# Pair scores from 32 sums and differences and a constant matrix, on two row groups of the array

## The chip, the core and the metric

The kernel runs on one core of one Trainium2 chip. The metric is the device time of one execution in microseconds (us); less is better. The program names the engines as the profile does: PE is TensorE's matmuls, PEld its weight loads, ACT is ScalarE, DVE is VectorE, POOL is GpSimd, SP is SyncE.

## The reference

The input is x (4 batches of 12416 tokens of 128 channels), 32 inducing vectors and three weights. Attention goes twice through a small set of 32 vectors, and a gated block follows:

```python
h = mab(I, x)                      # 32 inducing rows attend to all tokens of a batch
return mab(x, h)                   # each token attends to the 32 rows of h
...
gate = np.maximum(x @ w_gate, 0.0)
val = x @ w_val
return gate * val @ w_out          # d_ff is 1536
```

Here `mab(q, kv)` is `softmax(q @ kv.T / sqrt(128)) @ kv`.

## The kernel before

**The algebra.** A token's attention weights p over the 32 rows of h are positive and sum to 1. Where the sign of each of the 1536 gates is the same for all tokens, the output is a quadratic form in p: a sum over pairs (k, m) of p_k p_m times a vector of 128 outputs. The product of two exponentials is the exponential of the sum of two scores. So the kernel takes 16 x 32 = 512 sums of two rows of h (`hs`), computes 512 pair scores for each token by a matmul of x with `hs`, exponentiates them (F), and multiplies F by a table T of 512 rows. A further set of 16 sums and 16 differences of rows (`h2`, made by `halves`, L125) gives 32 more exponentials per token (`p2`), which meet rows 512 and up of T: the fifth product. A column of T adds up the softmax's denominator. A guard, `general_kernel`, does the plain computation where the signs are not certain; it isn't run on these inputs.

**Tiles.** A batch has 97 token tiles of 128, which form 24 blocks of four tiles (512 tokens) and one tile more. Four blocks make a chunk: six chunks and the last tile.

**Stages.** `first_batch` (L153) loads x of batch 0, transposes it on PE, and computes h. Then comes a hand-written order of gates, products and tables of batch 0 (L940 to L969). After it one loop over all 4 x 97 tiles (L1004) emits everything else. For each block: two score units (`scores`, L555), each two matmuls of 128x512 into the two halves of an `e_ps` tile (L581) and one exponential of 128x1024 on ACT (L588). For each token tile: four products of F with T and the fifth product, all into one third of an `o_ps` bank (`outputs`, L592: L602, L606). After three tiles, DVE takes the reciprocal of the denominators (L621) and scales the rows into `osb` (L622), and POOL stores six tiles by one DMA (L632). [...] two `e_ps` tiles of two banks, two `o_ps`, and two of tag "m" for all else.

For each chunk `mix_p` (L641) computes the 32 scores for four blocks by four matmuls on four column groups (`s2_pe`, L366), exponentiates them on ACT into `p2`, and lets DVE find their largest value (L646). `bound1` to `certain` use it for the guard.

**The next batch.** Between these, the loop does the first attention of the next batch: loads of x (POOL's queue), transposes by DMA (SP's queue) or, for three chunks of batch 1, by PE with a DVE copy (`turn_pe`, L722), scores and sums (L731, L740), h, the gates (`gates_pe`, L340; `gates_out`, L353), products U on DVE (L465), and five tables (L514, L533).

**What sets the order.** There is no scheduler at run time: each engine executes its instructions as they were emitted. The loop at L1003 keeps an estimated clock of each engine and emits next what it thinks can start first: a score unit (`emit_scores`), a side step (`emit_side`) from one of the lanes "phase", "units" and "scores", each with a place measured in half blocks and estimated costs, or the next output tile (`emit_tile`). Loads, transposes and stores are tied to the start of a block (`dmas`). Score units may run up to eight blocks ahead of the outputs (eight F buffers of 4x512).

Of the kernel before, what the change touches and what calls it, by code (L numbers as in the profile page):

```python
# [26 lines left out]
def quadratic_body(ctx, tc, x, inducing, moe_w_gate, moe_w_val, moe_w_out, out):  # L27
# [4 lines left out]
    P = 128  # L32
# [41 lines left out]

    T = [constp.tile([P, 8, P + 2], FP16, name=f"T{i}") for i in range(2)]
# [45 lines left out]
    def new_range(b):  # L121
        state[b]["rng"] = mt([P, 7], FP32, "rng", 2)
        nc.gpsimd.memset(state[b]["rng"], 0.0)

    def halves(b, h_ps, z_ps):  # L125
# [6 lines left out]
        h = s["h"] = st([P, M + NS], FP32, "h", 2)  # L132
# [20 lines left out]
    def first_batch(sp, psum):  # L153
# [30 lines left out]
        warm = mt([P, BLK], FP16, "p2", 14)  # L184
# [42 lines left out]
        new_range(0)  # L227
# [20 lines left out]
        def score(j):  # L248
            t0, t1 = parts[j]
            n = t1 - t0  # L250
            ps = bank("g", "s1_ps", [P, 8, M])
            tile = mt([P, BLK], FP16, "p2", 14)
            if j == 0:
                nc.vector.memset(tile[:, n * M : 8 * M], 0.0)
            for t in range(n):
                nc.tensor.matmul(ps[:, t, :], xTs(xT, t0 + t, 1), indT, start=True, stop=True)  # L256
            p1s[j] = tile[:, 0 : 8 * M].rearrange("p (t m) -> p t m", m=M)
            nc.scalar.activation(  # L258
                out=p1s[j][:, 0:n, :], in_=ps[:, 0:n, :], func=AF.Exp, scale=sm_scale
            )  # L260
# [65 lines left out]
    def h_sums(b):  # L326
        s = state[b]
        s["hs"] = st([P, NS, M], FP16, "hs", 2)
        h = s["h"]
        dve.tensor_copy(out=h[:, M : M + NS], in_=h[:, 0:NS])  # L330
        a = h[:, 0:M]
        wins = bass.AP(a.tensor, a.offset, [a.ap[0], (1, NS), (1, M)])
        dve.tensor_tensor(
            out=s["hs"],
            in0=h[:, 0:M].unsqueeze(1).broadcast_to([P, NS, M]),
            in1=wins,
            op=ALU.add,
        )

    def gates_pe(b, w):  # L340
        ps = bank("e", "hw_ps", [P, 2, BLK])
        for t in range(NFF):
            k, i = divmod(t, NFF // 2)
            nc.tensor.matmul(
                ps[:, k, i * (M + NS) : (i + 1) * (M + NS)],
                w[:, t * P : (t + 1) * P],
                state[b]["hT"],
                start=True,
                stop=True,
            )  # L350
        return ps

    def gates_out(eng, ps, dst, k):  # L353
# [4 lines left out]
        to = dst.rearrange("p (k i) m -> p k i m", k=2)[:, :, :, 0:n]  # L358
# [20 lines left out]
    def bound1(b):  # L379
# [3 lines left out]
        dve.tensor_reduce(out=v, in_=s["rng"], axis=AX.X, op=ALU.max)  # L383
# [130 lines left out]
    def table(b, j):  # L514
# [5 lines left out]
        dve.tensor_copy(out=T[b % 2][:, j, 0:P], in_=ps)  # L520
# [31 lines left out]
    F, p2s, osbs = {}, {}, {}  # L552
    dmas = defaultdict(list)

    def scores(g, half):  # L555
        b, n = divmod(g, NSLOT)
        s = state[b]
        hs = s["hs"].rearrange("p k m -> p (k m)")
        ps = bank("e", "e_ps", [P, 2, BLK])
        if n == NBLK:  # L560
            F[g] = mt([P, 4, BLK], FP16, "F", 8)
            for j in range(4):
                nc.tensor.matmul(
                    ps[:, 0, j * P : (j + 1) * P],
                    hs[:, j * P : (j + 1) * P],
                    xTs(s["xT"], NT - 1, 1),
                    start=True,
                    stop=True,
                )
            act.activation(  # L570
                out=F[g][:, :, 0:P],
                in_=ps[:, 0, :].rearrange("p (j c) -> p j c", j=4),
                func=AF.Exp,
                scale=sm_scale2,
            )
            return
        if half == 0:
            F[g] = mt([P, 4, BLK], FP16, "F", 8)
        for d in range(2):
            j = 2 * half + d  # L580
            nc.tensor.matmul(  # L581
                ps[:, d, :],
                hs[:, j * P : (j + 1) * P],
                xTs(s["xT"], n * TPB, TPB),
                start=True,
                stop=True,
            )
        act.activation(  # L588
            out=F[g][:, 2 * half : 2 * half + 2, :], in_=ps, func=AF.Exp, scale=sm_scale2
        )  # L590

    def outputs(b, t):  # L592
        i = t % 3
        n, tt = divmod(t, TPB)
        g = b * NSLOT + n
        if i == 0:
            outputs.ps = bank("o", "o_ps", [P, 3, P + 1])
        ps = outputs.ps[:, i, :]
        r = n % 4
        tok = slice(tt * P, (tt + 1) * P)  # L600
        for j in range(4):
            nc.tensor.matmul(  # L602
                ps, F[g][:, j, tok], T[b % 2][:, j, 0 : P + 1], start=j == 0, stop=False
            )
        rows = slice(0, P if n < NBLK else M)
        nc.tensor.matmul(  # L606
            ps,
            p2s[b, n // 4][rows, tok],
            T[b % 2][rows, 4 + r, 0 : P + 1],
            start=False,  # L610
            stop=True,
        )
        done = i == 2 or t == NT - 1
        if done:
            k = i + 1
            a = t - i
            if a % 6 == 0:
                osbs[0] = mt([P, 6, P], FP32, "osb", 4)
            osb, a6 = osbs[0], a % 6
            rz = mt([P, 3, 1], FP32, "rzo", 4)  # L620
            dve.reciprocal(out=rz[:, 0:k, :], in_=outputs.ps[:, 0:k, P : P + 1])  # L621
            dve.tensor_tensor(  # L622
                out=osb[:, a6 : a6 + k, :],
                in0=outputs.ps[:, 0:k, 0:P],
                in1=rz[:, 0:k, :].broadcast_to([P, k, P]),
                op=ALU.mult,
            )
            if a6 == 3 or t == NT - 1:
                t0 = a - a6
                last = b == B - 1 and t >= NT - 8  # L630
                queue = pool if not last else act if t == NT - 1 else nc.sync
                store = lambda: queue.dma_start(  # L632
                    out=ov[b][:, t0 : t + 1, :], in_=osb[:, 0 : t + 1 - t0, :]
                )
                if last:
                    store()
                else:
                    dmas[g + 1].append(store)
        return done

    def mix_p(b, q, later=False):  # L641
        ps = bank("m", "s2_ps", [P, BLK])
        k, w = s2_pe(b, q, ps)
        p2 = p2s[b, q] = mt([P, BLK], FP16, "p2", 14)
        act.activation(out=p2[0:k, 0:w], in_=ps[0:k, 0:w], func=AF.Exp, scale=sm_scale2)  # L645
        reach = lambda: dve.tensor_reduce(  # L646
            out=state[b]["rng"][0:k, q : q + 1],
            in_=ps[0:k, 0:w],
# [4 lines left out]
        if later:  # L653
            return reach
        reach()


# [7 lines left out]
    def charge(steps, tag=None, after=0.0):  # L665
        t = after
        if tag:
            i = taken[tag] % 2
# [10 lines left out]
    lanes = {"phase": [], "units": [], "scores": []}  # L679
# [7 lines left out]
    def plan_scores(b):  # L687
        h0 = 2 * NSLOT * b
        for q in range(0 if b else 1, NCH):
# [3 lines left out]
                h0 - 3 + 2.5 * q,  # L693
                lambda q=q: mix_p(b, q),
                [("PE", 0.32 * w), ("ACT", 0.5 * w), ("DVE", 0.64 * w)],
                "m",
                ("p2", b, q),
                [("h", b)],
            )
        later("scores", h0 + 15, lambda: bound1(b), D(0.6), None, ("b1", b))  # L700
        later(
            "scores",
            h0 + 16,
# [6 lines left out]
        later("scores", h0 + 17, lambda: certain(b), D(0.5), None, ("certain", b), [("A", b)])  # L710

    def plan_phase1(b):
# [9 lines left out]
        def turn_pe(q, k):  # L722
# [6 lines left out]
            dve.tensor_copy(out=s["xT"][q][:, 8 * k : 8 * k + 8, :], in_=ps)  # L729
# [54 lines left out]
        def h_end2():  # L784
            halves(b, s["h_ps"][:, 0, :], s["h_ps"][:, 1, :])
            new_range(b)
# [14 lines left out]
        if b == 1:  # L801
            moved["in"], moved["turn"] = 4.0, 0.0
            dmas[0] += [lambda q=q: turn(q) for q in turns[0:4]]
            for h in range(6):
# [4 lines left out]
                    [("PE", 0.47), ("DVE", 0.7)],  # L809
# [34 lines left out]
        def gates(w, a, odd, eng, eng2):  # L844
            ps = gates_pe(b, w)
            gates_out(eng, ps, a, 0)
            gates_out(eng2, ps, odd, 1)

        later(
            "phase",  # L850
            c + 2,
            lambda: gates(wg, ga, gb, act, act),
            [("PE", 0.35), ("ACT", 0.65), ("ACT", 0.65)],
            "e",
            ("g", b),
            [("h", b), ("T", b - 1)],
        )
        later("phase", c + 2.5, f(h_sums), D(0.86), None, ("hs", b), [("h", b)])
        later(
            "phase",  # L860
            c + 3.5,
            lambda: gates(wv, va, vb, dve, act),
            [("PE", 0.35), ("DVE", 0.7), ("ACT", 0.65)],
            "e",
            ("v", b),
        )
# [21 lines left out]
        for j, k in enumerate(ends):  # L888
            todo.append(
                (place(k) + 1.5, f(table, j), [("PE", 0.7), ("DVE", 0.3)], "m", ("T", b, j), [("U", b, k)])  # L890
# [27 lines left out]
    done.update({("h", 0): 0.0, ("hs", 0): 0.0, ("T", 0): 0.0, ("p2", 0, 0): 0.0})  # L918
# [3 lines left out]
    for b in range(B):  # L922
# [4 lines left out]
        2 * (n_all - NSLOT) + 20,  # L927
# [8 lines left out]
    def all_k(t0):  # L936
        for i, odd in ((0, 0), (1, 0), (1, 1), (0, 1)):
            products(i, t0, 3, 0, NS, odd)

    ps = gates_pe(0, wg)  # L940
    gates_out(act, ps, ga, 0)
    ps2 = gates_pe(0, wv)
    gates_out(act, ps2, va, 0)
    gates_out(act, ps, gb, 1)
    gates_out(act, ps2, vb, 1)
    h_sums(0)
    gate_sum(0, 0)
    signs(0)
    reach = mix_p(0, 0, True)
    all_k(0)  # L950
    masked_act(0, 0, 3)
    scores(0, 0)
    masked_act(0, 3, 3)
    scores(0, 1)
    table_all(0, 0, 3)
    masked_act(0, 6, 6)
    scores(1, 0)
    all_k(3)
    table_all(0, 3, 3)
    scores(1, 1)  # L960
# [5 lines left out]
    table5(0)  # L966
    table_all(0, 9, 3)
    scores(2, 0)
    reach()  # L969


    NF = 8
# [289 lines left out]
```

## Time and profile before

| what | value |
|---|---|
| median of 6 runs | 303.12 us (299.46 to 306.18) |
| the profiled execution's own time | 299.69 us |
| its span, first to last instruction | 297.6 us |
| mean granted TensorE clock | 0.996 |
| first score exponential starts, last one starts | 27.9 us, 280.7 us |
| last fifth product starts | 290.7 us |
| moved by DMA | 48.37 MB |

In a row of a group, the numbers behind the bar are the time in which the engine was busy with the group and the mean length of one instruction in ns, then the idle time ahead of the group and what ended most of it. A row of the timeline has the start, the length from the first start to the last end, and the number of instructions merged into it. Matmuls overlap, so the length of one is not the time between two.

The span in 40 slices of 7.4 us:

```
PE   4997999999897999998999999989999999999991
DVE  3659865547886776778967763669988655664571
ACT  3337899997984778997877889799777889979800
DMA  7999969697979984997999521212423232222253
```

### The profile page before, as it was taken

The page shows a single profiled execution, that of the slowest core. Times are in us where ns is not written, and L with a number is a line of the kernel's source. Part 1 is how long each engine was busy: PE and PEld are TensorE (multiplying, and loading weights), DVE is VectorE, ACT ScalarE, POOL GpSimd, SP SyncE. Part 2 cuts the span into 40 slices and gives each one's busy share as a digit, 9 for nine tenths or more (in the row PEclk, how much of TensorE's full clock was granted, in tenths as well). Part 3 has the DMA queues.
Part 4 walks back from the last instruction along what each step waited for, and adds up shares of the span by engine and source line. Part 5 has one row for each costly group of instructions (what it writes and reads, how often), then busy time and mean ns, then how long its engine had stood idle before and what let it go on. Part 6 is the DMA issues. An engine that isn't in the chain of part 4 may idle for free.

```text
span 297.6 us, 9408 instructions
## 1 busy us (share of the span) xinstructions
PE 275.9 (93%) x4029; PEld 206.5 (69%) x4029; DVE 202.6 (68%) x561; ACT 228.1 (77%) x290; POOL 61.9 (21%) x134
## 2 busy tenths in 40 slices
PE   4997999999897999998999999989999999999991
PEld 2884877677666787765777787666778776667790
DVE  3659865547886776778967763669988655664571
ACT  3337899997984778997877889799777889979800
POOL 7461000223211013311302012011211121121220
PEclk9999999999999999999999999999999999999998
DMA  7999969697979984997999521212423232222253
GB/s 181 202 208 207 215 90 245 126 226 142 260 212 233 179 186 122 208 265 222 220 173 285 177 108 64 106 57 107 161 86 129 107 118 109 103 111 108 106 214 126
DMA packets 44433, 48.37 MB, mean 163 GB/s; under 512 B 35472, under 2 KB 36272, under 8 KB 44384
## 3 DMA queue, kind: packets, MB, share of 16 engines
q0 software_dynamic: 11936, 38.08, 47.1%
q1 hardware_dynamic: 32160, 9.16, 18.0%
q8 instruction: 33, 0.54, 0.8%
q10 hardware_dynamic: 288, 0.46, 0.5%
q14 instruction: 16, 0.13, 0.1%
HBM read 27.80 MB, written 25.43 MB: 179 GB/s over the span
## 4 chain that ended last, share of the span: by engine, by line
PE 61%; ACT 17%; DMA 10%; DVE 7%; issue 2%; SPq 0%; POOL 0%; ACTq 0%; DVEq 0%; POOLq 0%
PE o_ps L602 23%; PE e_ps L581 19%; ACT F L588 15%; PE o_ps L606 5%; DMA x<-in_x_dram 5%; DMA x16r<-in_x_dram 3%; PE T_ps L517 3%; DVE U L471 2%; PE s_ps L736 2%; DMA xT<-x 2%; PE hz_ps L757 2%; PE s_ps L370 2%; DVE osb L622 1%; ACT p L645 1%; PE T_ps L537 1%
## 5 line engine op out<-in xcount | busy, mean ns | idle before, releaser
L588 ACT ACTIVATE F<-e_ps 128x1024 f16<-128x1024 f32 x192 | 187.3, 1031 | 29.7 <-PE e_ps L581 27.7
L602 PE MATMUL o_ps<-T,F 128*128 128x129 f16 x1552 | 132.0, 221 | 1.9 <-DVE osb L622 1.6
L602 PEld LDWEIGHTS <-F 128*128 128x128 f16 x1552 | 106.1, 98 | 31.4 <-issue 4.8
L581 PE MATMUL e_ps<-xT,hs 128*128 128x512 f16 x384 | 106.2, 378 | 2.8 <-ACT gb L360 1.7
L606 PE MATMUL o_ps<-T,p 128*128 128x129 f16 x388 | 84.6, 218 | 0.0
L632 POOL DMA_DIRECT2D out_dram<-osb x65 | 35.5, 546 | 205.7 <-DVE osb L622 148.6
L622 DVE TENSOR_TENSOR osb<-o_ps,rzo 128x384 f32<-128x384 f32 x132 | 72.5, 549 | 4.5
L581 PEld LDWEIGHTS <-hs 128*128 128x128 f16 x384 | 32.1, 97 | 22.5 <-issue 8.2
L621 DVE RECIPROCAL rzo<-o_ps 128x3 f32<-128x3 f32 x132 | 23.1, 175 | 27.2 <-PE o_ps L606 25.7
L606 PEld LDWEIGHTS <-p 128*128 128x128 f16 x388 | 37.9, 98 | 0.4
L646 DVE TENSOR_REDUCE rng<-s_ps 128x1 f32<-128x512 f32 (+1 forms) x28 | 17.7, 631 | 20.2 <-ACT p L645 20.2
L645 ACT ACTIVATE p<-s_ps 128x512 f16<-128x512 f32 (+1 forms) x28 | 15.9, 569 | 1.7 <-PE s_ps L370 1.6
L738 ACT ACTIVATE p<-s_ps 128x512 f16<-128x512 f32 (+1 forms) x21 | 11.8, 577 | 3.9 <-PE s_ps L736 3.8
L258 ACT ACTIVATE p<-s_ps 128x256 f16<-128x256 f32 (+3 forms) x16 | 5.3, 332 | 10.5 <-PE s_ps L256 10.5
L736 PE MATMUL s_ps<-indT,xT 128*128 128x32 f16 x288 | 10.0, 177 | 2.5 <-DMA xT<-x 2.3
L246 DVE COPY xT<-xT_ps 128x1024 f16<-128x1024 f16 (+2 forms) x15 | 8.8, 584 | 5.2 <-PE xT_ps L245 3.8
L736 PEld LDWEIGHTS <-xT 128*128 128x128 f16 x288 | 9.0, 96 | 3.0 <-DMA xT<-x 2.5
L480 DVE TENSOR_TENSOR U<-U,U 128x1536 f16<-128x1536 f16 (+1 forms) x12 | 10.8, 903 | 0.2
L85 POOL DMA_DIRECT2D x<-in_x_dram x18 | 9.8, 551 | 2.1 <-PE s_ps L256 1.3
L768 DVE TENSOR_TENSOR hz<-hz,hz_ps 128x129 f32<-128x129 f32 (+1 forms) x18 | 5.2, 288 | 7.2 <-PE hz_ps L757 6.8
L517 PE MATMUL T_ps<-wo,U 128*128 128x128 f16 x144 | 10.0, 219 | 0.0
L370 PE MATMUL s_ps<-xT,h 128*32 128x512 f16 x96 | 9.6, 389 | 0.0
(153 smaller groups left out, 241.5 us busy)
## 6 DMA issues: line engine op xcount, KB each, us to landing
out_dram<-osb POOLq DMA_DIRECT2D x62, 384.0 KB, 3.3
x<-in_x_dram POOLq DMA_DIRECT2D x18, 512.0 KB, 9.9
x<-in_x_dram POOLq DMA_DIRECT2D x8, 256.0 KB, 7.6
out_dram<-osb SPq DMA_DIRECT2D x2, 384.0 KB, 2.9
x<-in_x_dram POOLq DMA_DIRECT2D x5, 128.0 KB, 8.4
osb<-in_x_dram ACTq DMA_DIRECT2D x1, 384.0 KB, 4.5
osb<-in_x_dram SPq DMA_DIRECT2D x1, 384.0 KB, 4.3
wg<-in_moe_w_gate_dram POOLq DMA_DIRECT2D x1, 384.0 KB, 8.3
```

What stands on the lines that cost most here:

```text
L370: nc.tensor.matmul(ps[32 * r : 32 * r + 32, 0:w], state[b]["h2"], xTs(state[b]["xT"], (4 * q + r) * TPB, w // P), start=True, stop=True,)
L517: nc.tensor.matmul(ps, u_cols(0, t, j), wo[:, t, :], start=t == 0, stop=t == NFF - 1)
L581: nc.tensor.matmul(ps[:, d, :], hs[:, j * P : (j + 1) * P], xTs(s["xT"], n * TPB, TPB), start=True, stop=True,)
L588: act.activation(out=F[g][:, 2 * half : 2 * half + 2, :], in_=ps, func=AF.Exp, scale=sm_scale2)
L602: nc.tensor.matmul(ps, F[g][:, j, tok], T[b % 2][:, j, 0 : P + 1], start=j == 0, stop=False)
L606: nc.tensor.matmul(ps, p2s[b, n // 4][rows, tok], T[b % 2][rows, 4 + r, 0 : P + 1], start=False, stop=True,)
L621: dve.reciprocal(out=rz[:, 0:k, :], in_=outputs.ps[:, 0:k, P : P + 1])
L622: dve.tensor_tensor(out=osb[:, a6 : a6 + k, :], in0=outputs.ps[:, 0:k, 0:P], in1=rz[:, 0:k, :].broadcast_to([P, k, P]), op=ALU.mult,)
L632: store = lambda: queue.dma_start(out=ov[b][:, t0 : t + 1, :], in_=osb[:, 0 : t + 1 - t0, :])
L645: act.activation(out=p2[0:k, 0:w], in_=ps[0:k, 0:w], func=AF.Exp, scale=sm_scale2)
L646: reach = lambda: dve.tensor_reduce(out=state[b]["rng"][0:k, q : q + 1], in_=ps[0:k, 0:w], axis=AX.X, op=ALU.max, apply_absolute_value=True,)
L736: nc.tensor.matmul(ps[:, t, :], s["xT"][q][:, t, :], indT, start=True, stop=True)
```

## The change

The pair scores come no longer from x. With a and b the sums and differences of rows (the 32 scores that `s2_pe` computes), the sum of two row scores is a fixed combination of them. So:

- a constant matrix `sel` (128 x 16 x 32, fp16; the same 32 rows four times) is built once, ahead of the warming matmuls, and takes the place of `hs`;
- `mix_p` falls into `pair_scores` (the four column matmuls), `pair_out` (DVE clamps the scores to +-64 and copies them to SBUF as fp16, `sc`, then finds the largest of that copy) and `pair_exp` (ACT, which now reads `sc`);
- a score unit is now a quarter j of the pairs for two blocks: two matmuls with 32 rows each, on row groups 2d and 2d+1, into the two halves of `e_ps`. F is kept in 16 buffers of 2x512;
- the fifth products of three tiles are emitted together after their twelve others, and, where a score unit is ready then, narrow (32 rows, on the row group of their block) between its two matmuls and its exponential. Otherwise they come as before, on all 128 rows;
- the gates go through "m" banks in halves, even columns copied by ACT and odd ones by DVE; the copies of PE transposes and of table parts move from DVE to ACT; the planner has a lane "exps" and other places and costs.

```diff
+        half = mt([P, M + NS], FP32, "half", 1)
+        for k, op in ((0, ALU.add), (1, ALU.subtract)):
+            nc.vector.tensor_tensor(
+                out=half[:, k * H : (k + 1) * H], in0=stackI[:, 0:H], in1=stackI[:, H:M], op=op
+            )
+        nc.vector.tensor_scalar(
+            out=half[:, 0:M], in0=half[:, 0:M], scalar1=0.5, scalar2=1.0, op0=ALU.mult, op1=ALU.mult
+        )
+        nc.vector.tensor_copy(out=half[:, M : M + NS], in_=half[:, 0:H])
+        windows(sel, half)
-        warm = mt([P, BLK], FP16, "p2", 14)
+        warm = mt([P, BLK], FP16, "p2", 6)
...
-        dve.tensor_copy(out=T[b % 2][:, j, 0:P], in_=ps)
+        act.copy(out=T[b % 2][:, j, 0:P], in_=ps)
...
-    def scores(g, half):
...
-        for d in range(2):
-            j = 2 * half + d
-            nc.tensor.matmul(
-                ps[:, d, :],
-                hs[:, j * P : (j + 1) * P],
-                xTs(s["xT"], n * TPB, TPB),
...
+    def scores(b, q, d, j, within=None):
         ps = bank("e", "e_ps", [P, 2, BLK])
+        sc = scs[b, q]
...
+        for r in range(0 if q == NQ else 2):
+            rows = slice(32 * (2 * d + r), 32 * (2 * d + r) + 32)
+            nc.tensor.matmul(ps[:, r, :], sel4[rows, j, :], sc[rows, :], start=True, stop=True)
+        if within:
+            within()
...
+        F[b, q, d, j] = mt([P, 2, BLK], FP16, "F", NF)
+        act.activation(out=F[b, q, d, j], in_=ps, func=AF.Exp, scale=sm_scale2)
...
+    def fifth_one(b, u, narrow, stop):
+        n, q, r, tok = place_of(u)
+        rows = slice(32 * r, 32 * r + 32) if narrow else slice(0, P if n < NBLK else M)
+        nc.tensor.matmul(
+            outputs.ps[:, u % 3, :],
+            p2s[b, q][rows, tok],
+            T[b % 2][rows, 4 + r, 0 : P + 1],
+            start=False,
+            stop=stop,
+        )
...
+    def fifths(b, t):
+        us = range(t - t % 3, t + 1)
+        blocks = [u // TPB for u in us]
+        main = max(set(blocks), key=blocks.count)
+        wide = [u for u in us if u // TPB != main]
+        for u in wide:
+            fifth_one(b, u, False, False)
+        rest = [u for u in us if u // TPB == main]
+        return rest, lambda narrow: [fifth_one(b, u, narrow, u == rest[-1]) for u in rest]
...
+    def pair_out(b, q, kw, ps):
+        (k, w), s = kw, state[b]
+        sc = scs[b, q] = mt([P, BLK], FP16, "sc", 3)
+        dve.tensor_scalar(
+            out=sc[0:k, 0:w], in0=ps[0:k, 0:w], scalar1=64.0, scalar2=-64.0, op0=ALU.min, op1=ALU.max
+        )
+        if q == 0:
+            s["reach"] = mt([P, NCH], FP32, "reach", 2)
+            pool.memset(s["reach"], 0.0)
+        dve.tensor_reduce(
+            out=s["reach"][0:k, q : q + 1],
+            in_=sc[0:k, 0:w],
...
+    def pair_exp(b, q):
+        k, w = (P, BLK) if q < NQ else (M, P)
+        p2s[b, q] = mt([P, BLK], FP16, "p2", 6)
+        act.activation(
+            out=p2s[b, q][0:k, 0:w], in_=scs[b, q][0:k, 0:w], func=AF.Exp, scale=sm_scale2
+        )
...
-            dve.tensor_copy(out=s["xT"][q][:, 8 * k : 8 * k + 8, :], in_=ps)
+            act.copy(out=s["xT"][q][:, 8 * k : 8 * k + 8, :], in_=ps)
...
+        def gates(w, a, odd, k):
+            ps = bank("m", "hw_ps", [P, BLK])
+            gates_pe(b, w, k, ps)
+            units = slice(k * (NFF // 2), (k + 1) * (NFF // 2))
+            gates_out(act, ps.unsqueeze(1), a[:, units, :], 0)
+            gates_out(dve, ps.unsqueeze(1), odd[:, units, :], 1)
...
+        t_e = unit_ready(begun)
+        rest, issue = fifths(b, t)
+        clock["PE"] += 0.06 * (i + 1 - len(rest))
+        if t_e > clock["PE"] + WAIT or units[e_at][1] == NQ:
+            issue(False)
+            clock["PE"] += 0.06 * len(rest)
+        else:
+            emit_scores(lambda: issue(True))
+            e_at += 1
+        outputs_end(b, t)
```

## The prediction

> **What bounds the kernel now.** I read the shares of busy time first, then the chain that ended last, the costliest groups, the table of waits, and last the timeline of TensorE alone.
>
> ```profile
> PE 275.9 (93%) x4029; PEld 206.5 (69%) x4029; DVE 202.6 (68%) x561; ACT 228.1 (77%) x290; POOL 61.9 (21%) x134
> ...
> PE 61%; ACT 17%; DMA 10%; DVE 7%; issue 2%; SPq 0%; POOL 0%; ACTq 0%; DVEq 0%; POOLq 0%
> ...
> L588 ACT ACTIVATE F<-e_ps 128x1024 f16<-128x1024 f32 x192 | 187.3, 1031 | 29.7 <-PE e_ps L581 27.7
> L602 PE MATMUL o_ps<-T,F 128*128 128x129 f16 x1552 | 132.0, 221 | 1.9 <-DVE osb L622 1.6
> L581 PE MATMUL e_ps<-xT,hs 128*128 128x512 f16 x384 | 106.2, 378 | 2.8 <-ACT gb L360 1.7
> L606 PE MATMUL o_ps<-T,p 128*128 128x129 f16 x388 | 84.6, 218 | 0.0
> ```
>
> TensorE carries 61% of the chain, and ScalarE's exponentials wait for it (27.7 us), hardly ever the reverse. Busy PE is not its price, because matmuls overlap. The price is the step from one start to the next, which the merged rows of the timeline give (row length less the mean of one, by the count less one):
>
> ```profile
> 43.52 0.59 PE L581 MATMUL e_ps<-xT,hs 128*128 128x512 f16 x2
> 44.05 0.40 PE L370 MATMUL s_ps<-xT,h 128*32 128x512 f16 x4
> 44.38 0.41 PE L602 MATMUL o_ps<-T,F 128*128 128x129 f16 x4
> 44.63 0.22 PE L606 MATMUL o_ps<-T,p 128*128 128x129 f16 x1
> ...
> 290.41 0.40 PE L602 MATMUL o_ps<-T,F 128*128 128x129 f16 x4
> 290.74 0.23 PE L606 MATMUL o_ps<-T,p 32*128 32x129 f16 x1
> ```
>
> A 512-column step is 0.59 - 0.378 = 0.215 us; an output product is (0.40 - 0.221)/3 = 0.059, a fifth product 0.056. Four 128*32 matmuls on four column groups take 0.40 together, so they run beside each other. The change of array shape has a price of its own: the second L581 starts at 43.735 and is streamed at 43.95, but L370 starts at 44.05; the last L370 starts near 44.06 and is streamed at 44.28, but L602 starts at 44.38. Each change costs about 0.10. The last row is the same for rows: the fourth L602 starts at 290.59, is through at 290.64, and the 32-row product starts at 290.74: 0.10 again.
>
> With these steps over the program's order TensorE needs 263 us of the 297.6 us span: 91.6 output products (1552 x 0.059), 82.6 scores (384 x 0.215), 21.9 fifths (388 x 0.0565), 10.4 for 104 changes of shape, and 56 for the rest. ScalarE, back to back, needs 220 (an exponential 0.93: ten of them stand in one row of 9.35 us). These two sums are close already.
>
> [...] No run here shows two row groups at once[...]
>
> **The change part by part.** Counts are from the built program's order.
>
> TensorE:
> - Scores: 384 full matmuls become 192 pairs on two row groups: 192 x (0.430 - 0.217) = -40.9. [...] I take 0.217.
> - Fifths: 257 of 388 come narrow inside a unit (105 units), 131 stay full. "A third row group beside them" holds only for 155 of the 257: the score unit runs ahead by a varying number of half chunks, and for 102 the fifth's own row group is one of the pair's, so it queues behind it. 155 x 0.0565 = -8.8. The 102 save nothing; if their weights also load exposed (0.098, the LDWEIGHTS row of L606), 43 units x 0.1 = +4.3; were they hidden too, -5.8. I take 0.
> - Changes of shape: 104 become 416, as nearly each unit goes in and out of row shape: 312 x 0.10 = +31.2. This eats most of the gain.
> - Sum -18.5 by these terms; the whole order costs 243.9 against 263.0, -19.1.
>
> ScalarE: six xT copies (128x1024, as an exponential, 0.93) +5.6; twelve table copies (128x128; L258's row of that shape has 0.277, of which 0.09 overlaps) +2.3; 28 pair exponentials now read SBUF[...]; nine gate copies of 0.65 become twelve halves of 0.42: -0.9. Sum +8: 220 becomes 228.
>
> VectorE: 28 clamped copies from PSUM (va's 576 elements take 0.753, so 512 take 0.69) +17.7; the reductions stay (0.69, from SBUF now); odd gate copies 12 x 0.45 = +5.4; setting up the matrix +1.3. Away: hs -3.5, xT copies -4.1, T casts -3.5, va -2.3. Sum +11: 214 of some 283 us, 76%, so it hides, except where it is the last link: a score unit now waits for PE s2, then DVE's copy. With three sc buffers the copy is placed about 7 blocks ahead, and output rows queue behind it for 1.4 us, while two o_ps banks cover 1.4 us (twice 12 products of 0.059). POOL's memset of reach now sits right ahead of the reduction, behind POOL's stores and loads; four times, 0 to 1 us each; I take 0.
>
> The start: the matrix is built ahead of the warming memset (3.64 us), so warm matmuls begin 1.3 later; the matmul queue is free again at about 7.1, not 5.8, where x's first cast ends at 5.9. Later the start waits for DMA (9.27 us in the chain from 8.1). Bounds 0 and 1.3; I take 0.7. The store, load and transpose DMAs keep their block and their order on POOL and SP; new is only that xT is no longer read by scores, so buffers free earlier.
>
> What the gain is worth: I added both engines over stretches of 12 score units, in both orders. From the 12th unit on, the larger of the two summed to 225.3 before, plus 8.5 of TensorE after the last unit; after the change it is 215.5 plus 3.0. So 19.1 shrinks to 15.3, since ScalarE is now the longer one in 8 of these 16 stretches (3 before). Before, the trace has 247.7 us for that part (43.3 to 291.0), that is 13.9 of waits over 233.8. With as many waits left the span is 297.6 - 15.3 + 0.7 = 283.0. Waits may grow, because in 12 of 16 stretches the two engines lie within 1 us of each other (8 of 16 before), each pair of e_ps banks is a hand-over, and three engines are near full: +0 to +18. They may shrink by up to 12: the 27.7 us that ScalarE waits would be fed by a faster PE. I take 0. The profiled run stood 2.1 us above its span: 285.1. The median of the runs shown is 1.1% above the profiled run's 299.69: 288.
>
> **Rivals.**
> 1. *ScalarE packs densely* (about 275). TensorE's spare time lets scores run just ahead, and ScalarE's 228 us bind: its gate copies start at 24.4, about 222 of its 228 follow, plus half of the old waits (14) and some 9 us of last products and stores: span near 270. For it: ten exponentials back to back at 35.87. Against: the same chain has whole batches of PE, tables and gates.
> 2. *The coupling takes it* (about 302). TensorE waits for a free e_ps bank in unit order, VectorE's copies delay the o_ps banks, and 15 us of new waits stand where TensorE's work was. For it: three sums of 244, 228 and 214. Against: the waits now are small, 0.5 for e_ps on ScalarE and 1.6 for o_ps on VectorE.
> 3. *Row groups don't run beside each other* (about 326; slower). A pair then costs 0.430: 192 x 0.213 = +40.9, the changes of shape stay, and TensorE's sum is 285 against 263: span near 320. It decides from a pair of 0.297 us on, where 192 x 0.08 uses up the 15.3. Against: four column groups share 0.40 us.
> 4. *The transfers bind*: the chain has 15.6 us of x loads and transposes from 75.28 to 91. Up to the 48th unit the stretch sums hardly change (73.4 before, 75.7 after), so batch 0 doesn't reach that wait earlier, and its extra 2.3 us may hide there. Within the range of the first case.
>
> **How the numbers follow.** My forecast (with 4 in it) has 0.65, with an own range of 280 to 297; rival 1 has 0.14, rival 2 0.13, rival 3 0.08. The range, 274 to 303, cuts most of rival 3 and the ends of 1 and 2. What this kernel can tell from no change is about 1% (300.1 to 306.2 here). Faster by over 1%: 0.65, 0.14 and a third of rival 2, 0.83 in all; within 1%: 0.08; slower: 0.09.
>
> **What would show it.** Two rows of L568 starting within 0.01 us, and the pair's step near 0.22: the pairing; 0.43 would be rival 3. The start of each unit 0.10 after the last product is through, likewise its end: changes of shape. Fifths within the pair's 0.38 us where the group is free, after it where not. ScalarE's share up from 77% to over 82%, and its wait for e_ps below 27.7 us. If that wait grows or o_ps waits on VectorE come to several us, rival 2. I am wrong in size if the changes of shape cost much less at row shape in a stream, or if waits move by over 10 us.

## The result, and the profile after

| | before | after |
|---|---|---|
| median of all executions | 302.51 us (71, 298.17 to 307.8) | 302.68 us (34, 296.28 to 310.63) |
| ratio after/before | | 0.9937, interval 0.9907 to 0.9967 |
| profiled execution, its span | 299.69, 297.6 us | 306.29, 304.3 us |
| mean granted TensorE clock of it | 0.996 | 0.922 |
| first reciprocal of batch 0 (end of the start) | 22.74 us | 23.74 us |

The ratio leaves out the slower executions of each kernel (27 of 39 after), so it isn't the quotient of the medians. The forecast of 288 us missed: the change gains 0.6% by this ratio and nothing by the medians, where 5% was forecast.

The clock row of the 40 slices before:

```profile
PEclk9999999999999999999999999999999999999998
```

The page of the kernel after, in the order of the page before: shares of busy time, the clock row, the chain, the groups.

```profile
PE 273.7 (90%) x4029; PEld 192.1 (63%) x4029; DVE 212.4 (70%) x577; ACT 234.5 (77%) x311; POOL 61.3 (20%) x134
...
PEclk9998799955599996579999999999999999999997
...
PE 63%; DVE 16%; ACT 13%; issue 5%; POOL 1%; POOLq 0%; ACTq 0%; DVEq 0%
...
L577 ACT ACTIVATE F<-e_ps 128x1024 f16<-128x1024 f32 x192 | 187.5, 1033 | 30.4 <-PE e_ps L568 29.0
L591 PE MATMUL o_ps<-T,F 128*128 128x129 f16 x1536 | 128.8, 228 | 5.0 <-DVE osb L628 3.7
...
L568 PE MATMUL e_ps<-sc,sel 32*128 32x512 f16 x384 | 76.5, 410 | 4.8 <-ACT won L457 2.4
...
L598 PE MATMUL o_ps<-T,p 32*128 32x129 f16 (+1 forms) x388 | 52.2, 224 | 0.0
```

The score matmuls (L568) take 76.5 us in place of 106.2, and the fifths 52.2 in place of 84.6; yet TensorE's busy time, in which overlapping groups count once, is only 2.2 us less. The chain has more PE than before, no DMA, and VectorE with 16%. ScalarE's wait for scores is 29.0 us, no shorter than the 27.7 before. And the row PEclk, which was 9 in all slices but the last before, has 5s, a 6 and some 7s: the granted clock fell to half for three stretches, 27.9 to 34.8, 62.1 to 82.6 and 116.7 to 133.8 us.

The timeline of TensorE at the place that the prediction used for its steps:

```profile
42.09 0.40 PE L591 MATMUL o_ps<-T,F 128*128 128x129 f16 x4
42.41 0.39 PE L568 MATMUL e_ps<-sc,sel 32*128 32x512 f16 x2
42.42 0.34 PE L598 MATMUL o_ps<-T,p 32*128 32x129 f16 x3
42.74 0.41 PE L591 MATMUL o_ps<-T,F 128*128 128x129 f16 x4
...
43.88 0.22 PE L598 MATMUL o_ps<-T,p 128*128 128x129 f16 x1
44.03 0.39 PE L568 MATMUL e_ps<-sc,sel 32*128 32x512 f16 x2
44.26 0.27 PE L598 MATMUL o_ps<-T,p 32*128 32x129 f16 x2
44.47 0.70 PE L591 MATMUL o_ps<-T,F 128*128 128x129 f16 x9
```

Everything that the prediction said of the array is there. At 42.41 two L568 start within 0.01 us and both are through in one length; three fifths start beside them at 42.42; the next full product starts 0.33 after the pair, which is 0.215 and a change of shape of 0.10. At 44.03 the fifths' row group is one of the pair's, and they start only when it is through, at 44.26.

So I split the time from each start on TensorE to the next into three: what the step costs at full clock by the prediction's prices, what half clock adds to it, and the rest, which is waiting. The split is an estimate: with slightly other prices its differences move by about 1 us.

| profiled run, us | own steps | half clock | waits | before the first and after the last matmul | span |
|---|---|---|---|---|---|
| before | 264.0 | 2.0 | 20.8 | 10.9 | 297.6 |
| after | 245.1 | 17.5 | 29.6 | 12.0 | 304.3 |
| difference (rounded) | -18.9 | +15.5 | +8.8 | +1.1 | +6.7 |
| forecast | -19.1 | 0 | +3.8 | +0.7 | -14.6 |

TensorE's own work shrank as forecast. It was given back by the clock, and by waits. The profiled run had a low clock; over the 39 executions of the kernel after whose clock is on record, the mean clock ran from 0.914 to 0.973 (mean 0.942), and a line through their times is 292.4 us + 181 x (1 - clock), with a correlation of -0.90. At 0.988, the mean of 44 executions of the kernel before, that gives 294.6; since no execution of the kernel after had a clock over 0.973, this is an extrapolation. By it, the clock took about 8.3 us of the median, and another 6 or so of the 14.7 us miss was there at any clock.

### The profile page after: what moved, and what is told of

Same layout as the page of the kernel before. It is cut to its first block, busy times and chain, and to the rows that moved or that the text cites. A ratio compares the mean times of both kernels' runs of the same rounds, so it can differ in the third digit from the quotient of the medians.

```text
span 304.3 us, 9528 instructions
## 1 busy us (share of the span) xinstructions
PE 273.7 (90%) x4029; PEld 192.1 (63%) x4029; DVE 212.4 (70%) x577; ACT 234.5 (77%) x311; POOL 61.3 (20%) x134
## 4 chain that ended last, share of the span: by engine, by line
PE 63%; DVE 16%; ACT 13%; issue 5%; POOL 1%; POOLq 0%; ACTq 0%; DVEq 0%
PE o_ps L591 25%; PE e_ps L568 14%; ACT F L577 10%; DVE osb L628 4%; PE o_ps L598 4%; DVE U L470 3%; PE T_ps L516 3%; PE s_ps L763 2%; PE hz_ps L784 2%; PE s_ps L369 2%; PE T_ps L502 2%; PE xT_ps L259 2%; DVE rzo L627 1%; ACT xT L756 1%; DVE sc L655 1%
## 5 line engine op out<-in xcount | busy, mean ns | idle before, releaser
L591 PE MATMUL o_ps<-T,F 128*128 128x129 f16 x1536 | 128.8, 228 | 5.0 <-DVE osb L628 3.7
L591 PEld LDWEIGHTS <-F 128*128 128x128 f16 x1536 | 94.8, 100 | 36.8 <-issue 19.4
L568 PE MATMUL e_ps<-sc,sel 32*128 32x512 f16 x384 | 76.5, 410 | 4.8 <-ACT won L457 2.4
L598 PE MATMUL o_ps<-T,p 32*128 32x129 f16 (+1 forms) x388 | 52.2, 224 | 0.0
L568 PEld LDWEIGHTS <-sel 32*128 32x128 f16 x384 | 18.5, 92 | 26.5 <-issue 8.7
L598 PEld LDWEIGHTS <-p 32*128 32x128 f16 (+1 forms) x388 | 28.9, 96 | 5.8 <-issue 1.4
L655 DVE TENSOR_SCALAR sc<-s_ps 128x512 f16<-128x512 f32 (+1 forms) x28 | 17.5, 626 | 3.9 <-PE s_ps L369 3.8
L765 ACT ACTIVATE p<-s_ps 128x512 f16<-128x512 f32 (+1 forms) x21 | 11.4, 548 | 10.4 <-PE s_ps L763 10.3
L661 DVE TENSOR_REDUCE reach<-sc 128x1 f32<-128x512 f16 (+1 forms) x28 | 17.6, 627 | 1.4 <-POOL reach L660 0.2
L672 ACT ACTIVATE p<-sc 128x512 f16<-128x512 f16 (+1 forms) x28 | 16.5, 589 | 0.0
```

Of the source, the lines that this page charges most:

```text
L568: nc.tensor.matmul(ps[:, r, :], sel4[rows, j, :], sc[rows, :], start=True, stop=True)
L591: nc.tensor.matmul(outputs.ps[:, i, :], f, T[b % 2][:, j, 0 : P + 1], start=i + j == 0, stop=False)
L598: nc.tensor.matmul(outputs.ps[:, u % 3, :], p2s[b, q][rows, tok], T[b % 2][rows, 4 + r, 0 : P + 1], start=False, stop=stop,)
L655: dve.tensor_scalar(out=sc[0:k, 0:w], in0=ps[0:k, 0:w], scalar1=64.0, scalar2=-64.0, op0=ALU.min, op1=ALU.max)
L661: dve.tensor_reduce(out=s["reach"][0:k, q : q + 1], in_=sc[0:k, 0:w], axis=AX.X, op=ALU.max, apply_absolute_value=True,)
L672: act.activation(out=p2s[b, q][0:k, 0:w], in_=scs[b, q][0:k, 0:w], func=AF.Exp, scale=sm_scale2)
```

## The experiments

Three readings of the clock were on trial. A: it follows how much of the array is streaming, so that a product on 32 rows counts for less than a full one. B: it follows gaps alone, in which TensorE streams nothing. C: it follows the number of waits and hand-overs, which the change raised.

**1. Streams of one shape.** TensorE alone; all of the reference's work is left out. Each stretch below follows one of 110 full products.

```
rows(110, (0,))                     # one row group, no gap
rows(110, (0, 1))                   # pairs on two row groups
strip(110)                          # 128x32, one column group
6 x (full(2), rows(16, (0,)))       # mixed
6 x (full(5), rows(13, (0,)))
```

> Only TensorE streams of 512 columns, one after the other, none of the reference's work: full array, one row group (32 rows), full, two row groups in pairs, full, one column strip (32 columns), full, six times 2 full and 16 of one row group, full, six times 5 full and 13 of one row group, full. Theory A (the granted clock follows the share of the array's cells that stream in windows of 3.41 us, and halves below about a third: in the profile of after the windows with 0.20, 0.30 and 0.31 were followed by half the clock, those with 0.36 and 0.37 were not): one row group (0.25 of the cells, without any gap) falls to 0.5, so does the strip (0.25); pairs (0.5) keep 1.0; 2 of 18 full (0.32 with the changes of shape) falls, 5 of 18 full (0.44) does not. Theory B (the clock falls where TensorE has too many gaps): 1.0 in all streams, since none has a gap.

The answer by stretches (from and to, the length, busy time of PE, PEld, VectorE and POOL with counts, then the granted clock):

```profile
7.00:31.00 24.00, 24.00 (x108) 10.59 (x106) 0.00 (x0) 0.00 (x0) 1.00 0.00 1
37.00:73.00 36.00, 36.00 (x86) 12.20 (x83) 0.00 (x0) 0.00 (x0) 0.50 0.00 0
99.00:123.00 24.00, 24.00 (x222) 10.66 (x222) 0.00 (x0) 0.00 (x0) 1.00 0.01 1
147.00:170.00 23.00, 23.00 (x108) 10.38 (x107) 0.00 (x0) 0.00 (x0) 1.00 0.00 1
...
205.00:241.00 36.00, 36.00 (x83) 10.70 (x82) 0.00 (x0) 0.00 (x0) 0.50 0.00 0
276.00:302.00 26.00, 26.00 (x61) 7.84 (x60) 0.00 (x0) 0.00 (x0) 0.50 0.00 0
```

PE is busy all the time in each. One row group alone (37 to 73) still ran at half clock (0.50), from 5.2 us after its start: B falls. Pairs on two row groups (99 to 123) kept full clock (1.00), 222 in the 24 us of 108 full products; 110 pairs took 23.91 us, so a pair costs 0.217, as forecast. A strip of 32 columns (147 to 170) kept 1.00 too, where A, which went by the cells of the array, had it fall: in these streams the columns in use don't count, the rows do. The second mix fell as well, which A had not expected, since I had counted its share of the array too high: in the 3.41 us before its drop the share weighted by rows is 0.36, not the 0.44 estimated.

That weighted share is worked out so: every matmul counts its columns at 0.213 us per 512 (half of the 0.427 between two warming products at half clock in the kernel before; at full clock they step at 0.215), times its rows over 128, and the sum is divided by 3.41 us; column groups side by side count once. The windows are counted off from a change of the granted clock, and "share" below means this share. The length 3.41 comes from the traces: each half-clock stretch before the end is a multiple of it (6.83, 20.48 and 17.07 us in the kernel after), and so are the full-clock stretches between them (27.31 and 34.13). Every granted clock on record in the profiles before and after is 0.50 or 1.00, and the first full one comes at 8.76 us before and at 10.88 after.

**2. Fill at the head.** Eleven full 128x512 products into an unused bank, where TensorE waits for the first gates.

```diff
+    fill_ps = bank("m", "fill_ps", [P, BLK])
+    for _ in range(11):
+        nc.tensor.matmul(fill_ps, eye16, xTs(state[0]["xT"], 0, TPB), start=True, stop=True)
```

> The changed kernel with eleven full 128x512 matmuls into an unused bank put behind the first batch's gates, where TensorE waits for 2.35 us before the first score unit. Theory A: the window from 24.5 us has about 0.7 of the array busy, the fall at 27.9 us goes (6.8 us at half clock), mean clock up by 0.01, span 3 us shorter than the changed kernel's at the same clock elsewhere: ratio to before 0.983 to 0.988. Theory B says the same, since a gap is filled. Theory C (hand-overs between the engines took the gain, the clock is a side show): ratio 0.993 as the changed kernel.

Median 296.75 us, ratio 0.9878 (0.9792 to 0.9964), profiled span 292.1. More work, less time. The first drop to half clock is gone, and of the other two one is left:

```profile
PEclk9999999957999999999999999999999999999997
```

The drop at 116.7 us is gone as well, with no fill near it. Why is open; the executions of one kernel differ in their drops (mean clocks of 0.960 to 0.976 here). The interval of the ratio also holds C's 0.993; what speaks against C here is the trace.

**3. The scores on all 128 rows.** The constant matrix is padded with zeros for each row group, and all fifths are full. The schedule, ScalarE and VectorE do as in the kernel after, but for four copies and memsets at the start.

```diff
-            nc.tensor.matmul(ps[:, r, :], sel4[rows, j, :], sc[rows, :], start=True, stop=True)
+            nc.tensor.matmul(ps[:, r, :], w[:, j, :], sc, start=True, stop=True)
```

> The changed kernel with each score matmul on all 128 rows (the constant matrix zero but for its 32 rows) and all fifths on 128 rows: no row shape in the loop, planner and order as in the changed kernel. TensorE's sum goes from 244 to about 264 us (+41 for the pairs, +9 for hidden fifths, -30 for changes of shape). Theory A: the clock stays above 0.985, and the time is 300 to 304, as before: 20 us more work for the same time as the changed kernel. Theories B and C: the clock stays at 0.93 to 0.96, where the gaps are the same, and the time rises to 312 or more.

Median 305.68 us, ratio 1.013 (1.0068 to 1.0193), clock 0.983 in the profile, with a drop only at the head. With the same order and hand-overs but 128 rows the main loop keeps its clock: against C. Its own steps were 264.7 us. Its waits were 22.5, though, nearer to the 20.8 before than to the 29.6 after, so this run alone doesn't part rows from waits; 4 and 9 do. The time is 1.7 us over the 300 to 304 that A gave.

**4. Row groups only where the fifth has a free one.** The other units on 128 rows, as in 3.

> The changed kernel, but a score unit uses the two row groups only where the fifths beside it have a row group of their own; all other units take 128 rows with the zero-filled matrix, and their fifths 128 rows. TensorE's sum should be within 5 us of 244, since a lone pair with two changes of shape costs 0.42 and two full matmuls 0.43. Theory A: the share of the array rises wherever lone pairs stood, clock 0.98 or more, time 288 to 293, ratio 0.955 to 0.97. Theory C: ratio 0.99 to 1.0.

Median 302.4 us, ratio 1.0007 (0.997 to 1.0044): a miss. The clock did rise (0.985 in the profile, 0.969 to 0.991 in all), but its own steps rose to 254.4 us and its waits stayed at 28.0. A kept clock alone isn't the forecast's gain. For the cause of the drops this run tells most: with waits of 28.0 us (29.6 after) and the same hand-overs, its profile has one drop before the end, at the head, so C falls.

**5. The matrix built later.** As 2, with the five instructions that build `sel` moved behind a transposed copy of the first batch.

> The version with eleven full fill matmuls behind the first gates (ratio to the kernel before 0.988, profiled span 292.1), and the constant matrix built between two transposed-x copies of the first batch instead of ahead of the warming memset. Theory A (the start is late by the matrix build alone): the first-batch reciprocal back from 23.74 to about 22.8 us, the span 1 us shorter at equal clock: ratio 0.983 to 0.987. Rival (the start is hidden behind a later wait, such as the transposes of batch 1): the reciprocal is earlier, the end is not: ratio 0.988, the wait of the first-phase scores for xT grows by 1 us.

Median 298.56 us, ratio 0.9801 (0.9715 to 0.9886). The first matmul starts 1.2 us earlier, as in the kernel before, but the first reciprocal came at 23.17 us; in version 2, with the matrix in its old place, it came at 22.97. The reciprocal goes with the time at which full clock is first granted (9.79 us here, 8.53 in 2, 10.88 in the kernel after). The build costs a few tenths, which these runs can't separate from that.

**6. Copies back on VectorE.** As 2, with the copies of transposed x and of tables on VectorE, as before the change (the planner's estimates follow).

```diff
-            act.copy(out=s["xT"][q][:, 8 * k : 8 * k + 8, :], in_=ps)
+            dve.tensor_copy(out=s["xT"][q][:, 8 * k : 8 * k + 8, :], in_=ps)
-        act.copy(out=T[b % 2][:, j, 0:P], in_=ps)
+        dve.tensor_copy(out=T[b % 2][:, j, 0:P], in_=ps)
```

> The version with the fill, but the transposed-x copies of batch 1 and the table copies go back to VectorE, as in the kernel before: ScalarE's sum 8 us shorter, VectorE's about 8 longer. Theory S (the added 8 us of TensorE waits come from ScalarE, which is the longer sum in half of the stretches): waits of TensorE fall by 2 to 5 us (28.7 in the fill version, 20.8 in the kernel before), ratio 0.972 to 0.982. Theory V (they come from VectorE, whose output rows free the o_ps banks late): the 3.7 us of o_ps waiting for osb grow, and the ratio is 0.99 to 1.00. Theory N (neither; the sums are only coupled): 0.985 to 0.991.

Median 302.09 us, ratio 0.9936 (0.9897 to 0.9975); waits 29.9 us. The table of TensorE's waits (what waited, on whom, us in all, times, longest):

```profile
PE o_ps L591 <- DVE osb L628: 6.4, 10, 1.9
```

It was 3.7 in version 2 and 1.6 in the kernel before. All waits are 1.2 us more than in version 2 (28.7), where theory S had 2 to 5 less: it falls. That the copies were well moved is likely, but the interval of the ratio overlaps that of version 2.

**7. A shorter reduction on VectorE.** As 2; the largest score is taken over 32 of 512 columns.

```diff
-            in_=sc[0:k, 0:w],
+            in_=sc[0:k, 0:32],
```

> The version with the fill, with the reduction of the largest pair score over 32 of its 512 columns (the rest of this bound is left out): VectorE loses 28 times about 0.5 us, 14 us in all, and nothing else changes. Theory V (VectorE's late output rows cause the added waits): o_ps waiting for osb falls from 3.7 to under 1.5 us, TensorE's waits from 28.7 to 24 to 26, ratio 0.974 to 0.981. Theories S and N: waits within 1 us of 28.7, ratio 0.985 to 0.991.

```profile
PE e_ps L568 <- ACT F L577: 3.0, 9, 0.6
...
PE o_ps L591 <- DVE osb L628: 1.2, 2, 0.7
```

The wait for VectorE fell from 3.7 to 1.2 us and all waits from 28.7 to 25.7, as theory V said. The ratio did not: 0.9874 (0.9802 to 0.9945), at clocks of 0.951 to 0.969. The profiled span was 294.9 us, in which half clock added 10.0 us, against 4.8 in version 2.

**8. No fifth beside a pair.** As 2, all fifths full and ahead of the pair.

```diff
-            emit_scores(lambda: issue(True))
+            issue(False)
+            emit_scores()
```

> The version with the fill, but every fifth product is a full one ahead of its pair, never on a row group beside it: 257 fifths at 0.0565 us are on TensorE's own time in place of 102, so its own sum grows by 8.7 us. If TensorE's own time sets the end: span up by 5 to 9 us, ratio 1.005 to 1.018. If waits fill the place anyway (coupling): TensorE's waits fall by as much as its work grows, span within 2 us, ratio 0.985 to 0.995. If the clock follows the share of active rows, it is not lower than the fill version's 0.96 to 0.976.

Median 298.56 us, ratio 0.9888 (0.9855 to 0.9922). TensorE's own steps rose by 9.8 us, its waits fell by 5.0 and half clock by 1.2; the span rose by 3.6. So in this pair of profiles half of a saving on TensorE turns into waits. The ratio is that of version 2 (0.9878) within the noise: fifths beside a pair gain nothing that these runs can tell.

**9. Fill where TensorE waits.** Version 5 with fill of 2 to 5 full products ahead of the first-phase scores of batch 1 and the first of batch 2, and 3 ahead of two tables. `fill` multiplies `eye16` by 512 columns of `wo`, into the bank that the step then overwrites.

```diff
+            fill(ps.rearrange("p t m -> p (t m)"), {(1, 3): 4, (1, 4): 2, (1, 5): 2, (1, 0): 4, (2, 0): 5}.get((b, q), 0))
...
+        fill(ps, 3 if b == 1 and j >= 2 else 0)
```

> The version with the late matrix and the head fill, plus fill at the places where TensorE waited in the other drops: 2 to 5 full 128x512 products ahead of the first-phase scores of batch 1 (and the first of batch 2), 3 ahead of the third and fourth table of batch 1, 4.95 us of TensorE in all if none falls into a wait, about 2.5 if half does. Theory A (the granted clock is set by the row-weighted share of streaming in each 3.41 us; it drops below about 0.36 to 0.37): no drop between 10 and 285 us in most runs, granted clock over 0.985, median 290 to 293, ratio 0.960 to 0.972. Rival C (the drops come from waits and hand-overs, which stay as they are): clock 0.94 to 0.97 as before, and the fill's own time on top: ratio 0.985 to 1.00. If the waits of 28 us stay, the span is 287 to 290.

```profile
PEclk9999999999999999999999999999999999999997
```

Median 296.21 us (292.35 to 309.23), ratio 0.9732 (0.9662 to 0.9802), the best ratio of all kernels here; by its median it is level with version 2 (296.75). The profiled execution, 292.61 us, has no drop from 7 to 287 us (clock 0.994). Its own steps are 251.3 us, some 4 of them fill; half clock adds 1.3, waits are 27.1. It doesn't hold the clock each time: six executions ran from 0.963 to 0.996, and only two over 0.985, so the expected median of 290 to 293 was missed, and most of the gain is that of the executions that keep it. The stretches of the two long drops, first in the kernel after, then here (columns as in 1, with ScalarE after VectorE):

```profile
62.00:82.00 20.00, 20.00 (x220) 12.02 (x212) 7.93 (x26) 13.75 (x16) 2.71 (x5) 0.50 0.54 118
...
117.00:133.00 16.00, 16.00 (x182) 9.33 (x171) 8.15 (x19) 11.87 (x15) 3.46 (x7) 0.50 0.51 117
```

```profile
62.00:82.00 20.00, 19.43 (x311) 13.64 (x304) 14.07 (x41) 19.67 (x26) 4.35 (x8) 1.00 1.00 214
117.00:133.00 16.00, 15.18 (x234) 10.43 (x222) 12.04 (x36) 15.73 (x22) 3.85 (x8) 1.00 1.02 224
```

PE is busy without a break in the first pair, and that is the trap: 220 matmuls in 20 us instead of 311, and ScalarE gets 16 instructions instead of 26.

**10. The kernel before with the same fill** (without the one at the head).

> The kernel before with the same fill in the first phase of batches 1 and 2 and the tables (no head fill). Its clock is 0.976 to 0.997 as it is. Theory A: few drops are there to be removed (mean clock 0.988), so the clock gains 0.005 to 0.008, worth 2 us, and the fill costs 2 to 5: ratio 0.995 to 1.01. Rival (any kernel gains from the fill, whatever its row shapes): ratio 0.97 to 0.985.

Median 303.99 us, ratio 1.0065 (1.0031 to 1.0099). Fill alone isn't a gain; here it was one only where the clock is lost.

**11. The bound itself.** TensorE alone, none of the reference's work; a set share of streaming after each full stretch, with products of four columns as spacers (they step at 0.025 us: 39 rounds of the first line took 18 us, and a full product 0.215 of each).

```
50 x (full(1), full(10, 4))
36 x (full(1), full(18, 4))
96 x (rows(1, (0, 1)), rows(1, (0,), 4))
66 x (rows(1, (0, 1)), rows(5, (0,), 4))
```

> TensorE alone, none of the reference's work: after each stretch of 110 full 128x512 products (23.7 us) comes a stretch of about 24 us with a set share of streaming, made with products of 4 columns as spacers (taken as 0.02 to 0.033 us each[...]). Theory A (what counts is the share of streaming in 3.41 us weighted by the rows in use, with the bound at 0.36 to 0.37): one full product and 10 spacers, weighted share 0.39 to 0.51: full clock stays; one full and 18 spacers, 0.26 to 0.37: falls to half; a pair on two row groups and 1 spacer, 0.42 to 0.45: stays; a pair and 5 spacers, 0.28 to 0.34: falls, though something streams for 0.56 to 0.68 of the time. Rival D (what counts is that anything streams, whatever its rows): the last one stays at full clock. Rival E (a pair counts as a full array): the last one stays too, with 0.56 to 0.68.

```profile
36.00:54.00 18.00, 18.00 (x429) 13.36 (x426) 0.00 (x0) 0.00 (x0) 1.00 0.01 4
88.00:108.00 20.00, 20.00 (x426) 13.93 (x424) 0.00 (x0) 0.00 (x0) 0.50 0.01 2
136.00:155.00 19.00, 19.00 (x242) 9.16 (x238) 0.00 (x0) 0.00 (x0) 1.00 0.01 2
...
190.00:214.00 24.00, 24.00 (x305) 11.92 (x302) 0.00 (x0) 0.00 (x0) 0.50 0.01 2
```

All four went as A said. The weighted shares from the trace: 0.48 to 0.52 stayed, 0.38 fell, pairs at 0.44 stayed, pairs at 0.32 fell, although in that last case something streams for twice that share, about 0.64 of the time (an estimate from the 0.32, in which a pair counts half). D and E fall. Over the kernels of this study the highest weighted share in a window that was followed by a drop is 0.384 (here), else 0.369; the lowest that kept its clock is 0.355, in the kernel before. Between these two the measure doesn't decide; the bound lies there, at about 0.36 to 0.38.

**12. Version 9 with the shorter reduction of 7.**

> The filled version with the late matrix (profiled span 290.5, TensorE's waits 27.1 us, clock 0.994; ratio 0.973), with the reduction of the largest pair score over 32 of 512 columns, the rest of this bound being left out. Theory V (about 3 us of the added waits are output rows that VectorE frees late): waits 23.5 to 25 us, span 287 to 288.5 at a clock over 0.985, ratio 0.962 to 0.968. Theory N (the waits move elsewhere): span within 1 us of 290.5, ratio 0.970 to 0.976.

```profile
PE s_ps L776 <- DMA xT<-x: 3.6, 1, 3.6
PE e_ps L580 <- ACT F L589: 3.0, 9, 0.6
...
PE o_ps L603 <- DVE osb L640: 1.2, 2, 0.7
```

Median 296.83 us, ratio 0.9857 (0.9812 to 0.9903): a miss, and by its median no better than 9. The wait for VectorE fell as in 7, but TensorE stood 3.6 us, until 94.7 us, for a transposed chunk of batch 2 that a DMA had not brought (0.2 in the profile of 9), and from 94.1 us the clock was at half for 6.83 us. One profile shows this; the mean clock of its six executions ran from 0.978 to 0.991.

## Why the prediction was wrong

**The steps of the array were right.** A pair costs 0.217 us (experiment 1); in the prediction this was the author's estimate, with no run behind it. A change of shape costs 0.10 each way, at 418 changes in the trace. Free fifths hide, conflicting ones queue: in the profile after, units with a pair and no fifth are followed by a full product after 0.320 us, with three free fifths after 0.322, with two conflicting ones after 0.434. The sum came to -18.9 against -19.1. Rival 3 (no concurrency) is refuted by experiment 1.

**ScalarE and VectorE were right within a few us.** The table copies and the transposed copies took 0.277 and 1.048, the clamped copy 0.685, the reduction 0.686; an exponential that reads SBUF 0.639 on average against 0.622 before. For 28 of them that makes 0.5 us; of the forecast's +8 for ScalarE 7.0 came from numbers of the trace, and the rest, for these exponentials, had no run behind it. VectorE rose by 9.8 us of busy time, where +11 was forecast.

**The start was right in part by luck.** It is 1.0 us later in the profile, inside 0 to 1.3. But version 2, the same program up to there, came at 22.97, only 0.2 us later than before; the other 0.8 goes with a later grant of full clock (10.88 against 8.53 us), of which the prediction had nothing.

**The step that failed is that every duration was taken at the clock of the kernel before**, from "With these steps over the program's order TensorE needs 263 us" down to "With as many waits left the span is". The loss of clock stood at nothing, without a reason. None of the four rivals had a lower clock. The cause, shown by experiments 1, 3, 4, 9 and 11: what kept the clock in them goes by the weighted share (drops after at most 0.384), in which a pair on two of four row groups counts half, and a 32-row fifth a quarter. Each unit made narrow takes weighted streaming out of its window: two full score products give 0.43 us, a pair 0.21. In the kernel before only two windows between 12 and 285 us are under 0.45, at 0.355 and 0.426, and neither drops. After the change the first drop follows a window of 0.21 (the wait of 2.35 us for ScalarE's `won`), the next ones windows of 0.30 and 0.31. A drop then feeds itself: at half clock the window counts half, and full clock came back only in windows of at least 0.37, which at half clock means a full array streaming for three quarters of the time. So in the kernel after waits of 1.1 to 2.4 us are followed by 6.8 to 20.5 us at half clock; the longest stretch in the profiles of these kernels is 27.3 us (version 5, at a clock of 0.948). On the median half clock costs about 8 us; it is 15.5 in the profiled run.

**The waits were mis-sized.** The forecast let 3.8 us of the 19.1 go to the coupling with ScalarE; 8.8 went. Rival 2 had named the mechanism (15 us of new waits); 8.8 of them came, with its sign: ScalarE's wait for scores grew to 29.0 us and o_ps waits for VectorE to 3.7. That its time, 302, is nearly the measured one is luck: the clock took what its waits didn't. Of the 5 us beyond the forecast, output rows that VectorE frees late account for 2 to 3 (1.6 to 3.7 in the row of waits; experiment 7 took 2.5 of it away and 3.0 of all waits). The prediction's claim that two o_ps banks cover VectorE's 1.4 us held only in part. The other 2 to 3 us aren't settled: they are spread over first-phase scores that wait for ScalarE and hand-overs of e_ps. Experiment 8 gives a measure: of 9.8 us put on TensorE, 5.0 came out of the waits, in one pair of profiles. At that rate the 18.9 us that the change took off would leave 9.6 of new waits; 8.8 came.

**Rival 1** (ScalarE packs densely) is refuted: even in 9, at a clock of 0.994, ScalarE's exponentials wait 18.5 us for scores. **Rival 4** was not what held the kernel after (DMA left its chain), but it is next: in 9 DMA is back with 13% of the chain, and in the profile of 12 it took back what VectorE gave.

Together: 288 forecast, 8.3 for the clock, 5.0 for waits and 0.6 for the start and the steps make 301.9 of the 302.7 that were measured. The clock's term is that of the median and the others are those of one profile, so the agreement is rough.

## What to carry to other kernels

Before tiling matmuls to a part of the rows, work out for each 3.41 us of the busy and of the sparse stages the streaming weighted by rows in use; here waits of 1.1 to 2.4 us, in windows that came to 0.21 to 0.31, were followed by 6.8 to 20.5 us at half clock. Read the granted-clock row beside the busy row first: PE that is busy without a break at half clock (20.00 of 20 us at 0.50, from 62 us on in the kernel after) looks like a saturated engine. Full products into an unused bank at the waits were cheaper than the drop, but only where there was one (0.973 here, 1.007 on the kernel before).

## What the runs showed of the hardware

- A stream of 32-row products with no gap fell to half clock (experiment 1: 110 of them took 42.07 us, where 110 full ones took 23.91), and in the kernel after waits of 1.1 to 2.4 us were followed by half clock. Gaps alone don't tell it: the window at 87.27 us of the kernel before, with PE busy for 1.46 of 3.41 us (share 0.355), kept full clock, and the one at 113.28 us of the kernel after, busy for 2.15 (share 0.31), was followed by half.
- The columns in use didn't count where it was tried: 128x32 products on one column group kept full clock for 23.9 us.
- The clock goes with this kernel's spread: after, the time falls with the clock of the execution (correlation -0.90). Before it is less clear: -0.83 in one set of 44 executions, -0.92 in 11, -0.68 in 23 and -0.28 in 16.
